# Four coupled edits to a fused two-layer kernel: segment 0's attention by halves of its queries, two of its row tiles normed midway, memory sums by 32-column products, narrower masked k, and a new order

## The chip, the cores and the metric

The kernel runs on one core of one Trainium2 chip. The metric is the device time in microseconds; lower is better. Three runs of the kernel before gave 544.15, 544.17 and 544.77 us, so the median is 544.17 us. One more execution was profiled.

Names used below: PE is the tensor engine (PEld its weight loads), DVE the vector engine, ACT the scalar engine, POOL the GpSimd engine, SP the sync engine, which issues most DMAs. `us` is a microsecond.

## The reference, cut to what matters

Two layers of the same kind are run over 2048 rows of 512. Each is an attention with a compressive memory, and a gated feed-forward.

```python
def _A_ref(x, wq, wk, wv, wo, beta):          # H = 32 heads of 16, N = 4 segments of L = 512
    ...
    for s in range(N):
        logits = einsum('bhqd,bhkd->bhqk', qs, ks) * scale + mask      # causal inside the segment
        a_dot = einsum('bhqk,bhkd->bhqd', softmax(logits), vs)
        pq = phi(qs)                                                   # t + 1 for t > 0, else exp(t)
        a_mem = einsum('bhld,bhde->bhle', pq, M) / (einsum('bhld,bhd->bhl', pq, z)[..., None] + 1e-06)
        outs.append(g * a_mem + (1.0 - g) * a_dot)
        pk = phi(ks)
        M = M + einsum('bhld,bhle->bhde', pk, vs)
        z = z + einsum('bhld->bhd', pk)
    ...
    return o @ wo
def _B_ref(x, w_gate, w_up, w_down):
    return _gelu(x @ w_gate) * (x @ w_up) @ w_down
x = x + _A_ref(_layernorm(x), ...)
x = x + _B_ref(_layernorm(x), ...)
x = x + _A_ref(_layernorm(x), ...)
x = x + _B_ref(_layernorm(x), ...)
```

M is a 16 by 16 matrix for each head, so it is used block by block along a diagonal.

## The kernel before

**Steps.** `k` counts eight steps: k = 0 to 3 are the segments of the first layer, 4 to 7 those of the second. Step k has an `Att(k)` and an `Ffn(k)`. Segment k + 4 needs the feed-forward of step k, and memory goes from one segment to the next, so attention of later segments runs beside the feed-forward of earlier ones. All weights and x stay in SBUF.

**Attention.** Rows are normed (`Norm`): statistics of each of four row tiles (`st6`, `mv`), one scale for all four on POOL (`rs`), the normed tile `xn`, and its transpose into `xnT`, either by PE (`turn_item`, tiles in `BY_PE`) or by a DMA transpose on SP's queue. Projections give q, k (`kf`) and v, v with a column for the softmax's denominator (`vaug`). The 32 heads are four blocks `b` of eight; a block's heads of even and odd number (`par`) are told apart by masked copies of k, `kx` (`masked_copies`, L417 on DVE or POOL). Scores are taken in nine rounds for each block (`round_of`, `FULL`, `PAIRED`), 36 for each step, by row tiles of PE (L938). One exponential on ACT (L1398, 128x1024) serves two rounds' half; POOL masks the diagonal. A `flush_item` sums probabilities times v by column tiles of PE (L954) for one block and one parity. Behind it DVE turns the result (`byq`, L971), takes the reciprocal (`r`), scales (`ab`, L979), turns it back (`aT`, L986) and, from the second segment on, adds the part from memory (`amT`). When the four blocks are there, 16 products with `wo` are added to x (L1027), and the rows are normed again for the feed-forward (`xnTf`).

**Memory.** phi(k) is made on ACT, POOL and DVE (`e`, L745) and turned by DMA (`phik`). `upd_item` sums phi(k) times v: 16 products of 128 rows by 128 columns, of which only the blocks on the diagonal are used. DVE then multiplies by a mask `bd` into `mblk` and keeps the running sum in `macc`. The next segment takes `den` (`zcols`, 16 products 8 wide) and `num` (`mblk`, 16 products 128 wide) from it, scales (`am`, L820) and turns by DMA (`amT`).

**Feed-forward.** 14 tiles of `wg` (gate), gelu on ACT, 14 of `wu` (up), times gelu on DVE (L1092), and 14 products for each of four row tiles with `wd` (down), added to x. `gel_sb` also serves as `vaug` of step 0, and `wd_sb` holds q, k and masked k of step 0 until `w_down` is loaded over them; so the first gate tiles wait for step 0's memory sum, and seven loads of `wd` wait for step 0's scores.

**Order.** Every engine runs a fixed list of instructions. `order` writes it when the program is built: it keeps a clock for each engine, picks PE's next piece of work among the items that it believes ready by their due times, and posts the work that follows to DVE, ACT, POOL and SP. `POLICY` holds the weights of these choices. Where it finds nothing for PE it puts in a product of the constant tile `warm` (L476 or L471 with `warm`), and `FILL` such narrow products (L584) go ahead of each transpose by PE. Nothing of this is decided on the chip: there the engines only wait for each other's semaphores.

**Tiling modes of PE.** A product may use the whole array (128\*128), four column tiles (128\*32, four instructions side by side) or four row tiles (32\*128). `product` cuts a dense product into four column tiles when a flush stands near.

Of the kernel before, what the change touches and what calls it, by code (L numbers as in the profile page):

```python
# [12 lines left out]
ALU = mybir.AluOpType  # L13
# [18 lines left out]
VALUES = TPS * VW + 16  # L32
SCALE = DH ** -0.5
# [11 lines left out]
PAIRED = [(ki, P * ki, C, C * ki) for ki in range(TPS)]  # L45


def round_of(t):

    b, i = divmod(t, ROUNDS)  # L50
    if i == SHARED:
        return b, (0, 1), PAIRED, None
    par = int(i > SHARED)
    return b, (par,), FULL[i - par * (SHARED + 1)], DIAG[i - par * (SHARED + 1)]


BY_PE = {("xnTf", 0), ("xnTf", 1), ("xnTf", NK - 1)}
BANKS = 8
# [3 lines left out]
URGENT, SOON, NORMAL = -4.0, -1.5, 0.0  # L62
XN_BUFS = 4
BUFS = 6
FILL = 2
# [4 lines left out]
    flush_wait=31.348, piece_slack=5.108, kb_slack=25.115, mem_slack=-15.103, margin=2.314, qk_due=0.572,  # L70
    e_q=-1.218, e_k=1.714, exp_slack=-25.107, e_slack=9.023, phi_slack=17.383, gelu_slack=6.274,
    act_evict=8.464, first_evict=0.965, gate_step=0.061, up_due=-0.553, up_step=0.062, down_due=2.078,
    down_step=0.526, upd_due=0.786, kb_act=6.552, vz_slack=-10.454, x_dve=-0.565, v0_due=-1.4, x1_at=-45.234,
    x2_at=18.289, x3_at=24.819, x3_load=-3.83, direct=4, gelu_tiles=4, look=1.769, lag=0.5, wv_at=8.591,
    xn_pool=7.037, kb_pool=5.303, cut_pool=1.107, at_pool=10.661, pe_turns=2, gate_due=0.765, shun=0.534,
    col_gap=3.33, hold=8, early=4.123, starve=0.308, near=-1.576, cap=4, soon=9.685, columns=0)
# [15 lines left out]
class Engine:  # L92
# [24 lines left out]
    def serve(self, now):  # L117
# [9 lines left out]
        job = min((j for j in jobs if j[0] + self.LATENCY <= start + 0.03), key=lambda j: j[0] + j[1] + (  # L127
# [123 lines left out]
class Item:  # L251


    def __init__(self, due, ready, ops, done, kind, ps, after="start"):
        self.after = after
        self.due = due if callable(due) else lambda: due
        self.ready, self.ops, self.done, self.kind, self.ps = ready, ops, done, kind, ps
        self.posted = 0.0
# [27 lines left out]
def order(pol, nc, cst, seg, wrk, psp, A_x, A_wq, A_wk, A_wv, A_wo, A_beta, B_x, B_w_gate, B_w_up, B_w_down, out):  # L286
# [88 lines left out]

    tmp_e2 = cst.tile([P, H], F32, name="tmp_e2")
    cden = cst.tile([P, H], BF16, name="cden")
    macc = cst.tile([P, 4, P], F32, name="macc")
# [32 lines left out]
    def masked_copies(ready, slack, kx, kf, told):  # L411
# [4 lines left out]
        def vector(which, eng):  # L416
            return lambda: eng.tensor_scalar(out=kx[:, :, C * which:C * which + P], in0=kf, scalar1=masks[:, which:which + 1],  # L417
                                             scalar2=None, op0=ALU.mult)
# [6 lines left out]
        ck.dve.post(ready, slack, (Port(0.35), vector(0, nc.vector), None),  # L425
                    (Port(0.35), vector(1, nc.vector), told), taken=taken)
        ck.pool.post(ready, slack + pol.kb_pool, (Port(1.57, True), vector(0, nc.gpsimd), None),
# [50 lines left out]
    def soon(name, n=KT, part=1.0):  # L478

        t = ck.pe - 0.1 - ck.back  # L480
# [20 lines left out]
    class Norm:  # L501
        def __init__(self, key, tt0, tag, slack, free):
            self.key, self.tt0, self.tag, self.slack, self.free = key, tt0, tag, slack, free
            self.mv, self.n, self.left = None, 0, TPS
# [3 lines left out]

        def stats(self, j, ready):
            def emit():  # L510
                if self.mv is None:
                    self.mv = self.small("mv", 2)
# [3 lines left out]
            def told(t):  # L516
                self.n += 1
                if self.n == TPS:
                    self.scales(t)

            ck.dve.post(ready, self.slack, (0.66, emit, None),
                        (0.17, lambda: nc.vector.bn_aggr(out=self.mv[:, j, :], in_=self.st6[:]), told))  # L522

        def scales(self, ready):
            def first():
                self.ve = wrk.tile([P, TPS, 1], F32, tag="lnve", name="ve")
                nc.gpsimd.tensor_scalar(out=self.ve[:], in0=self.mv[:, :, 1:2], scalar1=EPS_LN, scalar2=None,
                                        op0=ALU.add)

            def second():  # L530
                self.rs = self.small("rs", 1)
                nc.gpsimd.tensor_tensor(out=self.rs[:], in0=self.ve[:], in1=mhalf[:], op=ALU.pow)  # L532

            ck.pool.post(ready, URGENT, (0.25, first, None),
                         (1.05, second, lambda t: ck.when(self.free, lambda: self.start(max(t, ck.pe)))))

        def start(self, ready):
            self.xnT = seg.tile([P, KT, L], BF16, tag=self.tag, bufs=1, name="xnT")
            for j in range(TPS):
                xn_slots.take(lambda n, j=j: bufs.take(lambda i: self.row(j, n, i, max(ready, ck.pe))))  # L540

        def normed(self, j, i, eng=nc.vector):
            xn = buffer(i, "xn")
            eng.tensor_scalar(out=xn[:], in0=x_sb[:, self.tt0 + j, :], scalar1=self.mv[:, j, 0:1],  # L544
# [3 lines left out]
        def row(self, j, n, i, ready):  # L548
# [13 lines left out]
            def told(t):  # L562
                if self.by_pe():
                    items.append(self.turn_item(j, xn, t, landed))
                else:
                    turn_later(t, self.slack, lambda: self.xnT[:, :, j * P:(j + 1) * P], lambda: xn()[:], landed,
                           pol.margin)

            on_dve_or_pool(ready, self.slack, pol.xn_pool if self.key[0] == "xnTa" else None, Port(0.405),
# [5 lines left out]
        def turn_item(self, j, xn, t, landed):  # L575
# [4 lines left out]
            def turned():  # L580
# [8 lines left out]
                        lambda: evict(ps, lambda: self.xnT[:, :, j * P:(j + 1) * P], turned, landed, URGENT),  # L589
# [937 lines left out]
```

## Time and profile before

| what | us |
|---|---|
| median of three runs | 544.17 |
| span of the profiled execution | 542.6 |
| PE busy | 527.1 |
| DVE busy | 443.1 |
| ACT busy | 434.4 |
| POOL busy | 305.9 |

How to read the rows that follow: a timeline row is start, duration, engine, line, operation, out<-in with rows\*columns of PE's tile and the moving operand's shape, and the count of merged instructions; in brackets stands idle time before it and what ended it. A group row has the count, then total busy us and mean ns of one, then the idle time before. A row of the view by stretch has the stretch, its length, and for each engine busy us and (x) instructions. The profiled execution's span leaves out what lies around the program's instructions, which the timed runs hold.

### The profile page before, as it was taken

To read this page: it belongs to the slowest core of one execution; us is meant where nothing else is said; L and a number is where in the kernel's file an instruction comes from. 1 tells how busy PE (TensorE), PEld (TensorE's weight loads), DVE (VectorE), ACT (ScalarE), POOL (GpSimd) and SP (SyncE) were. 2 spreads that over 40 slices of the span, in tenths; PEclk is the share of its full clock that TensorE was granted. 3 is DMA by queue.
4 is the path that set the end of the run, shared out by engine and by line. 5 is a ranking of instruction groups with operands and counts; after the bars stand their busy time and mean duration, and the time that the engine had idled before them with its cause. 6 is when DMAs were issued, how large, how long until landed. Compare 5 with 4: busy or idle time off the path is not lost.

```text
span 542.6 us, 21272 instructions
## 1 busy us (share of the span) xinstructions
PE 527.1 (97%) x9271; PEld 274.9 (51%) x9332; DVE 443.1 (82%) x816; ACT 434.4 (80%) x540; POOL 305.9 (56%) x359
## 2 busy tenths in 40 slices
PE   8999989999999999999999999999999999999997
PEld 4454455454545444544544555545465456555444
DVE  7898999799988999879987998889586797786342
ACT  6999989988998989989799798996879977930320
POOL 4897786369846788349993468716753265300000
PEclk9999999999999999999999999999999999999999
DMA  8306510610331123310312250211420105100001
GB/s 268 98 13 192 117 23 17 171 35 20 51 50 24 24 40 61 41 38 9 41 32 50 33 71 4 40 33 23 79 52 3 22 13 89 24 3 25 16 0 40
DMA packets 64784, 26.94 MB, mean 50 GB/s; under 512 B 49074, under 2 KB 64690, under 8 KB 64690
## 3 DMA queue, kind: packets, MB, share of 16 engines
q1 hardware_dynamic: 64400, 25.31, 22.7%
q8 instruction: 73, 1.20, 0.9%
q10 hardware_dynamic: 290, 0.26, 0.2%
q14 instruction: 21, 0.17, 0.1%
HBM read 9.70 MB, written 2.10 MB: 22 GB/s over the span
## 4 chain that ended last, share of the span: by engine, by line
PE 83%; DVE 12%; issue 2%; DMA 2%; ACT 0%; POOL 0%; SPq 0%; DVEq 0%; ACTq 0%
PE ps L476 44%; PE ps L471 25%; PE ps L938 7%; PE ps L954 6%; DVE st L514 2%; DVE x_sb L1027 1%; DVE xn L544 1%; DVE byq L971 1%; DMA phik<-e 1%; DVE phiq L745 1%; DVE mv L522 1%; DMA x_sb<-in_A_x_dram 0%; DMA amT<-am 0%; DVE e L745 0%; ACT pt L1398 0%
## 5 line engine op out<-in xcount | busy, mean ns | idle before, releaser
L1398 ACT ACTIVATE pt<-ps 128x1024 bf16<-128x1024 f32 x288 | 279.1, 1026 | 44.3 <-PE ps L938 40.3
L1345 POOL TENSOR_SCALAR_AFFINE_SELECT pt<-pt 128x256 bf16<-128x256 bf16 (+1 forms) x192 | 108.6, 579 | 117.1 <-ACT pt L1398 110.4
L1092 DVE TENSOR_TENSOR gel_sb<-gel_sb,ps 128x512 bf16<-128x512 bf16 x112 | 75.2, 681 | 34.0 <-PE ps L476 25.0
L476 PE MATMUL ps<-xnT,wu_sb 128*128 128x512 bf16 x287 | 66.8, 379 | 1.4 <-issue 1.1
L476 PE MATMUL ps<-xnT,wg_sb 128*128 128x512 bf16 x261 | 62.6, 379 | 1.3 <-issue 0.5
L764 POOL TENSOR_SCALAR e<-e 128x512 bf16<-128x512 bf16 x37 | 57.6, 1557 | 1.6 <-ACT e L741 0.6
L971 DVE STREAM_TRANSPOSE byq<-ps 128x512 f32<-128x512 f32 x64 | 45.0, 706 | 16.3 <-PE ps L954 15.6
L476 PE MATMUL ps<-wd_sb,gel_sb 128*128 128x512 bf16 (+1 forms) x293 | 56.8, 340 | 1.3 <-issue 1.0
L1027 DVE TENSOR_TENSOR x_sb<-x_sb,ps 128x512 bf16<-128x512 bf16 (+1 forms) x68 | 42.8, 640 | 16.5 <-PE ps L476 14.8
L1350 POOL TENSOR_SCALAR_AFFINE_SELECT pt<-pt 64x1024 bf16<-64x1024 bf16 x40 | 47.7, 1194 | 15.1 <-ACT pt L1398 13.8
L471 PE MATMUL ps<-wd_sb,gel_sb 128*32 128x512 bf16 (+1 forms) x792 | 47.1, 378 | 0.6 <-issue 0.6
L476 PEld LDWEIGHTS <-wu_sb 128*128 128x128 bf16 x301 | 28.3, 98 | 33.8 <-issue 0.7
L471 PE MATMUL ps<-xnT,wg_sb 128*32 128x512 bf16 x700 | 42.4, 380 | 0.1
L514 DVE BATCH_NORM_STATS2 st<-x_sb 128x6 f32<-128x512 bf16 x60 | 40.4, 673 | 0.1
L476 PEld LDWEIGHTS <-wg_sb 128*128 128x128 bf16 x273 | 25.3, 98 | 29.1 <-DVE byq L971 0.6
L476 PEld LDWEIGHTS <-gel_sb 128*128 128x128 bf16 x306 | 28.3, 98 | 22.6 <-issue 1.1
L954 PE MATMUL ps<-pt,vaug 128*32 128x256 bf16 (+2 forms) x1344 | 34.8, 238 | 0.3 <-POOL pt L1345 0.3
L471 PE MATMUL ps<-xnT,wu_sb 128*32 128x512 bf16 x588 | 34.1, 379 | 0.0
L417 POOL TENSOR_SCALAR kx<-kf,masks 128x512 bf16<-128x512 bf16 x20 | 33.0, 1649 | 1.2
L1151 ACT ACTIVATE gel_sb<-gel_sb 128x2048 bf16<-128x2048 bf16 (+1 forms) x21 | 33.2, 1643 | 0.0
L954 PEld LDWEIGHTS <-vaug 128*32 128x32 bf16 x1344 | 27.9, 97 | 10.5 <-issue 2.3
L544 DVE TENSOR_SCALAR xn<-x_sb,mv,rs 128x512 bf16<-128x512 bf16 x58 | 31.4, 592 | 2.2 <-POOL rs L532 1.9
(149 smaller groups left out, 877.0 us busy)
## 6 DMA issues: line engine op xcount, KB each, us to landing
vz<-vaug SPq DMA_DIRECT2D x14, 136.0 KB, 2.7
wg_sb<-in_B_w_gate_dram SPq DMA_DIRECT2D x8, 224.0 KB, 4.0
wu_sb<-in_B_w_up_dram SPq DMA_DIRECT2D x8, 224.0 KB, 5.0
wd_sb<-in_B_w_down_dram SPq DMA_DIRECT2D x7, 256.0 KB, 4.7
x_sb<-in_A_x_dram SPq DMA_DIRECT2D x3, 512.0 KB, 6.6
out_dram<-x_sb SPq DMA_DIRECT2D x12, 128.0 KB, 1.9
xnT<-xn SPq DMA_TRANSPOSE x40, 2.5
wk_sb<-in_A_wk_dram SPq DMA_DIRECT2D x2, 256.0 KB, 5.1
```

The source lines that it names most:

```text
L471: nc.tensor.matmul(out[r], lhsT=lhsT[:, r], rhs=rhs, start=start, stop=stop, tile_position=(0, 32 * c))
L476: nc.tensor.matmul(out, lhsT=lhsT, rhs=rhs, start=start, stop=stop)
L514: nc.vector.bn_stats(out=self.st6[:, 0, :], in_=x_sb[:, self.tt0 + j, :])
L764: lambda eng: eng.tensor_scalar(out=e[0][:], in0=e[0][:], scalar1=1.0, scalar2=None, op0=ALU.min), summed)
L938: nc.tensor.matmul(ps_all[:, bank, o + c0:o + c0 + n], lhsT=lhsT, rhs=self.q[rows, b, q0:q0 + n], start=True, stop=True, tile_position=(32 ...
L954: nc.tensor.matmul(ps()[32 * j:32 * j + 32, q0:q0 + n], lhsT=va[:, ki * VW + g:ki * VW + g + 32], rhs=pt_all[:, places[i], j, c0:c0 + n], ...
L971: nc.vector.transpose(out=self.byq[:, par, :, :].rearrange("p a c -> p (a c)"), in_=ps()[:])
L1027: ck.dve.post(ck.made(), slack, (0.15 + 0.00104 * (c1 - c0), lambda: nc.vector.tensor_tensor(out=xt, in0=xt, in1=ps()[:, 0:c1 - c0], op=AL ...
L1092: ck.dve.post(ck.made(), NORMAL, (0.683, lambda: nc.vector.tensor_tensor(out=g, in0=g, in1=ps()[:], op=ALU.mult), lambda t: (ps.read(t), e ...
L1345: nc.gpsimd.affine_select(out=view, in_=view, pattern=[[0, 4], [0, n], [1, C]], compare_op=ALU.is_ge, fill=0.0, base=C, channel_multiplier=-1)
L1350: nc.gpsimd.affine_select(out=view, in_=view, pattern=[[0, 4 * TPS], [1, C]], compare_op=ALU.is_ge, fill=0.0, base=0, channel_multiplier=-1)
L1398: nc.scalar.activation(out=pt_all[:, s0:s0 + 2, 2 * p:2 * p + 2, :].rearrange("p r h c -> p h r c"), in_=ps_all[:, pair[0]:pair[1] + 1, :] ...
```

## The change

1. **Segment 0's attention by halves of its queries** (`HALVED`, `table`). Block 0 is done as before. For blocks 1 to 3 the rounds are laid out anew: first the rounds whose queries are in the first 256 rows (`early`), then those of the second 256 (`late`), in the order of blocks 1, 2, 3 and 3, 1, 2; rounds of the pair of parities are shared between blocks. A flush now covers both parities of one block and one half, and its steps on DVE behind the whole turn are half as wide. `wo` of row tiles 0 and 1 needs the first halves alone (`aTh`).
2. **Two of its four tiles normed midway** (`QUICK`, `told`, `scales`). For the feed-forward of step 0, tiles 0 and 1 get their scale, `xn` and transposes as soon as the two are there, tiles 2 and 3 later. Tile 2 takes its mean from an accumulated row sum of the addition to x, and its variance from a square on ACT (`added`).
3. **Memory sums by 32-column products** (`upd_item`). For each of the 16 pairs of row tile and block, four products with 32 columns of phi(k) and 32 columns of v, side by side in the column tiles. `macc` shrinks to 32 columns a block; `spread` makes `mblk` out of it. In the first segment `macc` is now copied ahead of `mblk`, where `mblk` came straight from PSUM.
4. **Narrower masked k** (`masked_copies`). The first masked copy on DVE and POOL is 64 columns a tile, not 128; the other 64 were written over by the second.
5. **New order.** All values of `POLICY` are new (among them `margin`, which adds to the expected landing of a DMA transpose: 2.314 before, 0.058 now), `FILL` is 0, a priority `CHAIN` stands ahead of all others for step 0's last flush and the norms behind it, and gate tiles that do not share memory with step 0's v may be taken before its memory sum.

```diff
-PAIRED = [(ki, P * ki, C, C * ki) for ki in range(TPS)]
...
-def round_of(t):
...
-    b, i = divmod(t, ROUNDS)
...
+HALVED = (0,)
+BOTH = (0, 1)
+EARLY = [(1, 192, 64, 0), (0, 64, 192, 64)]
+LATE = [([(3, 448, 64, 0), (2, 320, 192, 64)], 2), ([(0, 256, 256, 0)], 0), ([(1, 256, 256, 0)], 0)]
...
+    def early(b):
+        return [([(b, (par,), *piece) for piece in EARLY], 2) for par in range(2)]
+
+    def late(b):
+        return [([(b, (par,), *piece) for piece in pieces], n) for pieces, n in LATE for par in range(2)]
+
+    for b in range(1 if halved else KT):
+        got, parts = whole_block(b)
+        at = add(got)
+        units.append((b, None, [((par,), [at[i] for i in range(i0, i1)]) for par, i0, i1 in parts]))
+    if halved:
+        a1, s12, a2 = add(early(1)), add([(shared((1, 0), (1, 1), (2, 0), (2, 1)), None)]), add(early(2))
+        a3, s3 = add(early(3)), add([(shared(*((3, ki) for ki in range(TPS))), None)])
+        units += [(1, 0, [(BOTH, [*a1, *s12])]), (2, 0, [(BOTH, [*a2, *s12])]), (3, 0, [(BOTH, [*a3, *s3])])]
+        units.append((3, 1, [(BOTH, [*s3, *add(late(3))])]))
+        l1 = add(late(1))
+        s12 = add([(shared((1, 2), (1, 3), (2, 2), (2, 3)), None)])
+        units += [(1, 1, [(BOTH, [*l1, *s12])]), (2, 1, [(BOTH, [*s12, *add(late(2))])])]
...
+QUICK = {("xnTf", k): (2,) for k in HALVED}
...
 XN_BUFS = 4
 BUFS = 6
...
-    flush_wait=31.348, piece_slack=5.108, kb_slack=25.115, mem_slack=-15.103, margin=2.314, qk_due=0.572,
...
+    flush_wait=3.781, piece_slack=153.679, kb_slack=116.912, mem_slack=-48.48, margin=0.058, qk_due=1.192,
...
-    macc = cst.tile([P, 4, P], F32, name="macc")
+    macc = cst.tile([P, 4, 32], F32, name="macc")
...
-            return lambda: eng.tensor_scalar(out=kx[:, :, C * which:C * which + P], in0=kf, scalar1=masks[:, which:which + 1],
-                                             scalar2=None, op0=ALU.mult)
+            n = P if which else C
+            return lambda: eng.tensor_scalar(out=kx[:, :, C * which:C * which + n], in0=kf[:, :, 0:n],
+                                             scalar1=masks[:, which:which + 1], scalar2=None, op0=ALU.mult)
...
+        def told(self, j):
+            def fn(t):
+                self.n += 1
+                if self.quick:
+                    self.pairs[j // 2] += 1
+                    if self.pairs[j // 2] == 2:
+                        self.scales(t, j // 2 * 2, 2)
+                elif self.n == TPS:
+                    self.scales(t, 0, TPS)
...
+            def add():
+                self.moments()
+                made.append(wrk.tile([P, 1], F32, tag="rowsum", bufs=4, name="rowsum"))
+                nc.vector.scalar_tensor_tensor(out=xt, in0=ps()[:], scalar=1.0, in1=xt, op0=ALU.mult, op1=ALU.add,
+                                               accum_out=made[0][:])
+
+            def mean():
+                nc.vector.tensor_tensor(out=self.mv[:, j, 0:2], in0=made[0][:].to_broadcast([P, 2]), in1=means[:], op=ALU.mult)
+
+            def square():
+                nc.scalar.activation(out=junk[:], in_=xt, func=ACT.Square, scale=float(D) ** -0.5, bias=self.mv[:, j, 0:1],
+                                     accum_out=self.mv[:, j, 2:3])
+
+            ck.dve.post(ck.made(), slack, (0.76, add, ps.read), (0.15, mean, lambda t: ck.act.post(
+                t, slack, (0.95, square, self.told(j)), table="exp")))
...
-            def m(c):
-                j, b = divmod(c, 4)
-                product(blocks()[:, b, :], self.phik[:, j, b * P:(b + 1) * P],
-                        by_head(self.vaug)[:, j, 4 * b:4 * b + 4, :, 0:DH], c == 0, c == n_mm - 1)
+            def m(j, b):
+                ck.tiling("columns")
+                for c in range(4):
+                    nc.tensor.matmul(pairs()[32 * c:32 * c + 32, b, :], lhsT=self.phik[:, j, b * P + 32 * c:b * P + 32 * c + 32],
+                                     rhs=by_head(self.vaug)[:, j, 4 * b + c, :, 0:DH], start=(j == b == 0),
+                                     stop=(j == TPS - 1 and b == 3), tile_position=(0, 32 * c))
...
+                def spread():
+                    nc.vector.tensor_tensor(out=made[0][:].rearrange("p b (c d) -> p b c d", d=32),
+                                            in0=macc[:].unsqueeze(2).to_broadcast([P, 4, 4, 32]),
+                                            in1=bd[:].rearrange("p (c d) -> p c d", d=32).unsqueeze(1).to_broadcast([P, 4, 4, 32]),
+                                            op=ALU.mult)
...
-                    steps = [(0.154, lambda: nc.vector.tensor_copy(out=zacc[:], in_=self.zk[:]), kept),
-                             (0.683, gated(blocks), None),
-                             (Port(0.2), z, told),
-                             (0.683, lambda: nc.vector.tensor_copy(out=macc[:], in_=blocks()), psm.read)]
+                    first = [(0.283, lambda: nc.vector.tensor_copy(out=macc[:], in_=pairs()), psm.read),
+                             (0.154, lambda: nc.vector.tensor_copy(out=zacc[:], in_=self.zk[:]), kept)]
...
+                ck.dve.chain(ck.made(), pol.mem_slack, *first, (Port(0.69), spread, None), (Port(0.2), z, told))
...
+            u, b, h, n, pars, used = flush
...
+            c0, c1 = (0, L) if h is None else (half * h, half * h + half)
+            na = (c1 - c0) // 32
+            work = []
+            for par in pars:
+                for t in used:
+                    for b2, par2, ki, q0, nq, o in TABLES[k][0][t][0]:
+                        if b2 == b and par in par2 and c0 <= q0 < c1:
+                            work.append((par, t, vz if len(par2) > 1 else self.vaug, ki, q0 - c0 + (par * half if h is not None else 0),
+                                         nq, o))
+            work.sort(key=lambda w: (w[0], w[3] if h is not None else w[2] is vz))
...
-                    nc.vector.transpose(out=self.byq[:, par, :, :].rearrange("p a c -> p (a c)"), in_=ps()[:])
+                    nc.vector.transpose(out=(self.byq[:, pars[0], :, :].rearrange("p a c -> p (a c)") if h is None else
+                                             self.byq[:].rearrange("p u a c -> p (u a c)")[:, 0:2 * na * 32]), in_=ps()[:])
...
-                    nc.vector.transpose(out=self.aT[:, b, :], in_=self.ab[b][:].rearrange("p a c -> p (a c)"))
+                    nc.vector.transpose(out=self.aT[:, b, c0:c1], in_=made[0][:, 0:na, :].rearrange("p a c -> p (a c)"))
...
-                return Item(k + 0.61 + 0.001 * j, lambda: soon(("aT", k)),
-                            dense(ps, pairs), done, kind="wo", ps=ps, after=("aT", k, 3))
+                return Item(k + 0.61 + 0.001 * j, lambda: soon(("aTh", k, j // 2), eager=k in HALVED),
+                            dense(ps, pairs), done, kind="wo", ps=ps, after=("aTh", k, j // 2, 3))
...
-                            lambda: ck.has(("xnTf", k)) and (("down", k - 1) if k else ("upd", 0)) in ev,
+                return Item(lambda: -0.8 if phase[0] == k else k + pol.gate_due + pol.gate_step * place(ft),
+                            lambda: ck.has(("xnTf", k)) and (k == 0 and ft >= HELD or (("down", k - 1) if k else ("upd", 0)) in ev),
```

One line of `POLICY` stands for all of them.

More of the change, by code (lines that the diff above doesn't have):

```diff
@@ L528, in first @@
                                         op0=ALU.add)
             def second():
[L531 to L539, printed above, removed]
+                if self.rs is None:
+                    self.rs = self.small("rs", 1)
@@ L1447, in order @@
                 got = [it for it in items if it.after in ev and it.ready() and (
-                    it.kind != "flush" or not streams or tight() or it.posted < late or ck.mode == "columns")]
+                    it.kind != "flush" or it.chain or not streams or tight() or it.posted < late or ck.mode == "columns")]
                 if got:
```

251 lines of the change are left out of this document (150 added, 101 removed).

## The prediction

> **What bounds the kernel now.** I read the page first: shares of the engines, the granted clock, the chain that ended last.
>
> ```profile
> span 542.6 us, 21272 instructions
> ...
> PE 527.1 (97%) x9271; PEld 274.9 (51%) x9332; DVE 443.1 (82%) x816; ACT 434.4 (80%) x540; POOL 305.9 (56%) x359
> ...
> PEclk9999999999999999999999999999999999999999
> ...
> PE 83%; DVE 12%; issue 2%; DMA 2%; ACT 0%; POOL 0%; SPq 0%; DVEq 0%; ACTq 0%
> ```
>
> TensorE is busy 97% of the span at the full granted clock, and 83% of the chain is PE. So the time is PE's instruction stream, plus the places where that stream waits. The second view, busy time by stretch, says where those are (columns: the stretch, then PE, PEld, DVE, ACT, POOL busy, the clock, DMA).
>
> ```profile
> 60.00:80.00 20.00, 17.89 (x426) 10.61 (x426) 19.49 (x41) 17.40 (x23) 15.63 (x18) 1.00 0.23 36
> ...
> 100.00:120.00 20.00, 19.48 (x408) 10.48 (x405) 19.23 (x36) 17.30 (x23) 9.85 (x13) 1.00 0.42 108
> 120.00:140.00 20.00, 18.35 (x365) 9.75 (x361) 19.53 (x39) 17.20 (x23) 17.40 (x20) 1.00 0.07 16
> ...
> 160.00:380.00 220.00, 216.83 (x4183) 110.96 (x4207) 192.39 (x343) 195.97 (x239) 140.77 (x160) 1.00 0.21 35
> ...
> 539.00:542.60 3.60, 0.46 (x5) 0.17 (x2) 0.42 (x1) 0.00 (x0) 0.00 (x0) 0.99 0.13 36
> ```
>
> From 160 to 380 us PE idles 3.17 of 220 us, 0.29 per 20, which is the ground level. It idles 2.11 us in 60 to 80, 0.52 in 100 to 120 and 1.65 in 120 to 140, and there DVE is nearly full. Only there can a better order win anything. The third view, PE's timeline, shows the first of these places.
>
> ```profile
> 70.74 0.28 PE L476 MATMUL ps<-gel_sb,phik 128*128 128x128 bf16 x2
> 71.38 0.60 PE L476 MATMUL ps<-gel_sb,phik 128*128 128x128 bf16 x7 [0.35 <-DMA phik<-e]
> ...
> 73.82 0.20 PE L938 MATMUL ps<-q,kf 16*128 16x64 bf16 x2
> 74.39 0.40 PE L938 MATMUL ps<-q,kf 16*128 16x64 bf16 x10 [0.37 <-ACT pt L1398]
> 74.72 0.51 PE L476 MATMUL ps<-warm 128*128 128x128 bf16 x6
> 75.16 0.52 PE L954 MATMUL ps<-pt,vaug 128*32 128x256 bf16 x16
> 76.00 0.30 PE L954 MATMUL ps<-pt,vaug 128*32 128x64 bf16 x8 [0.33 <-POOL pt L1345]
> ...
> 76.50 0.20 PE L938 MATMUL ps<-q,kf 16*128 16x64 bf16 x3
> 77.16 0.27 PE L938 MATMUL ps<-q,kf 16*128 16x64 bf16 x5 [0.45 <-DVE macc L893]
> ...
> 77.71 0.21 PE L584 MATMUL ps<-warm 128*128 128x32 bf16 x2
> 77.76 0.38 PE L586 MATMUL ps<-ident,xn 128*128 128x128 bf16 x4
> ```
>
> Segment 0's attention is done, its feed-forward needs the normed rows, and PE is filled with products of `warm`. Read from start to start (a record's own length hides part of a wait), the four breaks are worth about 0.5 to 0.6 us each; with the smaller ones the stretch loses 3.3 us. The stretch from 100 to 160, read the same way, loses 3.0. Sum 6.3 us, beside 29 whole-width `warm` products (0.22 us of wait for each; 0.17 in the first place alone).
>
> **The change, part by part.** PE's price list comes from four places of its timeline.
>
> ```profile
> 230.70 1.67 PE L476 MATMUL ps<-xnT,wu_sb 128*128 128x512 bf16 x7 [0.16 <-issue]
> 232.31 0.40 PE L938 MATMUL ps<-q,kx 32*128 32x256 bf16 x12
> 232.64 2.12 PE L476 MATMUL ps<-xnT,wu_sb 128*128 128x512 bf16 x9
> ...
> 288.41 0.69 PE L471 MATMUL ps<-zcols,phiq 128*32 128x8 bf16 x64
> 288.93 1.27 PE L471 MATMUL ps<-xnT,wu_sb 128*32 128x512 bf16 x20
> ...
> 395.11 1.19 PE L471 MATMUL ps<-vaug,phik 128*32 128x128 bf16 x64
> 396.07 0.65 PE L471 MATMUL ps<-wd_sb,gel_sb 128*32 128x512 bf16 x7
> ```
>
> *Memory sums.* Now 16 products, 128 wide, take 396.07 - 395.11 = 0.96 us. After it is 64 products of 32 columns of phi(k) with 32 columns of v, four at a time. The nearest row is `zcols`: 64 such products, 8 wide, in 0.52 us. So 0.5 each, and six sums save 6 x 0.46 = 2.8 us. Ends: 0.24 (the time of now by the columns, 128 to 32) and 0.96 (nothing saved): 4.3 to 0.
>
> [...]
>
> *Mode switches.* Every change between whole, column and row tiles costs time. 230.70 to 232.31 is seven products of 0.216 and 0.10; 232.31 to 232.64 is 0.22 of scores and 0.11. The changed kernel's instructions stand in 322 runs of one mode against 304: 18 x 0.11 = 2.0 us more (fewer dense products are cut into columns, since flushes stand differently).
>
> *Fills.* 31 `warm` products become 25, and the 24 narrow ones ahead of the transposes (`FILL`) go. 74.72 to 75.16 is six of them and a switch: 0.055 each; 77.71 to 77.76 is two narrow ones: 0.03 each. 6 x 0.055 + 24 x 0.03 = 1.0 us less.
>
> PE without waits: -2.8 + 2.0 - 1.0 = **-1.8 us**. The other columns streamed are the same in number.
>
> *Halved attention of segment 0.* Six units of half the queries take the place of three whole ones: as many turns of a whole bank, three more reciprocals, scales and turns back of half the size. This adds some 1.3 us to DVE beside PE's projections and is free there; without that cover it costs what it is. On the path is only the last unit.
>
> ```profile
> 62.59 0.70 DVE L971 STREAM_TRANSPOSE byq<-ps 128x512 f32<-128x512 f32 x1
> 63.32 0.35 DVE L975 RECIPROCAL r<-byq 128x32 f32<-128x32 f32 x1
> 63.71 0.69 DVE L979 TENSOR_TENSOR ab<-byq,r 128x512 bf16<-128x512 f32 x1
> 64.43 0.71 DVE L986 STREAM_TRANSPOSE aT<-ab 128x512 bf16<-128x512 bf16 x1
> ...
> L1199 ACT ACTIVATE pt<-x_sb,shift 128x512 bf16<-128x512 bf16 x1 | 0.7, 721 | 0.0
> ...
> L417 POOL TENSOR_SCALAR kx<-kf,masks 128x512 bf16<-128x512 bf16 x20 | 33.0, 1649 | 1.2
> ```
>
> That is 2.55 us now, and about 1.9 with the last three steps halved. In the changed order eight `wo` products stand before the last flush, and 2.2 us of other PE work between it and the other eight. So `wo` stops waiting. Tiles 0 and 1 are normed while PE still projects segment 3; only tile 3's statistics stay on DVE at the end, and tile 2's variance moves to ACT (0.72 by the row of the same operation at the start; at worst one exponential of 1.03 ahead of it). From the last `wo` to the first `wg` product there are 5.7 us of work in the changed order, against 7.3 now, 1.3 of it fills. I take 0.4 us of remaining wait (0 to 1.5). Of the 3.3 us lost there, 2.9 go.
>
> *Where the stall goes.* The 25 fills of the new order all stand in one place: behind the last `wd` product of the first feed-forward, ahead of segment 4's v products (the next layer), which are drawn forward into a hole. These v products wait for `xnT` of segment 4. In DVE's new order 13 instructions stand between the turn of segment 1's last flush but one and the first `xn` of it: the last add to x, its two of statistics, two of phi, the memory sum's four, a whole turn, reciprocal, scale, turn back. DVE does one in 0.53 us in the 100 to 120 stretch (19.23 / 36). With `xn`, and 0.3 left of the turn when the last `wd` product ends, that is 14 x 0.53 + 0.3 = 7.7 us; then one transpose by DMA, whose landing is on the page:
>
> ```profile
> xnT<-xn SPq DMA_TRANSPOSE x40, 2.5
> ...
> phik<-e SPq DMA_TRANSPOSE x24, 3.4
> ...
> wd_sb<-in_B_w_down_dram SPq DMA_DIRECT2D x7, 256.0 KB, 4.7
> ...
> L971 DVE STREAM_TRANSPOSE byq<-ps 128x512 f32<-128x512 f32 x64 | 45.0, 706 | 16.3 <-PE ps L954 15.6
> ...
> L745 DVE SCALAR_TENSOR_TENSOR phiq<-q,e 128x512 bf16<-128x512 bf16 x24 | 19.2, 807 | 0.4 <-POOL e L764 0.4
> ...
> L878 DVE TENSOR_TENSOR mblk<-macc,bd 128x512 bf16<-128x512 f32 x4 | 3.9, 970 | 0.0
> ```
>
> 7.7 + 2.5 = 10.2, plus 0.6 for the memory sum's own wait for `phik`, against 5.8 us of PE work in that place: 5.0 us of wait. Behind the v products stand a flush, segment 1's `wo` and segment 4's q and k, so all wait together. Ends: 0.17 us for each fill gives 4.2; if all the steps took as long as the three large kinds above (0.83 on average), 11.9 + 3.1 - 5.8 = 9.2. I stay near the lower end, since statistics, sums and reciprocals are short. The 3.0 us lost there before are part of this.
>
> *Small new waits.* The order keeps less room before DMA landings: segment 2's first gate product stands 13.2 us of PE work after its last `wo`, now 15.9. The last four loads of `wd` stand on SP's queue behind two transposes of `amT`, and the products that read them follow 8 to 10 us of PE work after those that the transposes wait for; such a load takes 4.7 us to land, after some 4 us of scaling and issuing. The first memory block has one more copy ahead of it on DVE. I take 0.8 us for these (0 to 3).
>
> *Free:* the masked k copies, 256 wide for 512 in the first half. POOL's 1.65 us (row above) becomes about 0.9; POOL is busy 56%, and only scores that stand later read them. A copy that were waited for would gain 0.7.
>
> Sum: -1.8 + (0.4 + 5.0 + 0.8) - 6.3 = **-1.9 us** on the profiled execution. Its span is 542.6; the runs' median of 544.17 has 1.6 us around it, and the tail behind the last product (the 3.6 us of the last stretch) is untouched. Forecast 544.2 - 1.9 = **542.3 us**.
>
> **The rivals.**
> - *The waits shrink more* (540.5): 4.2 us in the new hole, none elsewhere but 0.2: -1.8 + 4.4 - 6.3 = -3.7. For it: 160 to 380 shows how well a fixed order can run. Against: DVE is full there.
> - *What the order gains is given back* (544.6): 1.5 us of wait left at segment 0 and 2 us of small ones: -1.8 + 1.5 + 5.0 + 2.0 - 6.3 = +0.4. For it: DVE is not relieved, and gates still need all four tiles normed.
> - *The new hole grows* (546.7): DVE's chain before segment 4's `xn` at 0.77 us a step. The wait is then 0.3 + 10.8 + 3.1 - 5.8 = 8.4 us, `wd` comes 1 us late: -1.8 + 8.4 + 0.4 + 1.8 - 6.3 = +2.5. It decides from 8 us in that one place. For it: 0.81 and 0.97 in the rows above.
> [...]
>
> **How the numbers follow.** Forecast 0.40, more gain 0.25, given back 0.18, hole grows 0.15, narrow products 0.02. What a measurement can tell from no change is about 0.2%, 1.1 us: faster is below 543.1, slower above 545.3. Faster takes nearly all of the first (0.38), the second, and 0.03 of the third: 0.66. Slower takes 0.11 of the fourth, the fifth, and 0.02 of the third: 0.15. Same is the rest, 0.19. The range, 539.0 to 545.8, leaves out the far end of the gain and of the growing hole.
>
> **What would show it.** Right: a column-tiled memory sum in 0.5 us; 322 runs of one mode with 0.11 between; PE's idle time in 60 to 80 near the ground level; one hole of 4 to 6 us between 115 and 130 with DVE full. Wrong: narrow sums at 1 us; waits at the first `wg` or `wd` products; idle time over 0.5 us per 20 after 160.

## The result, and the profile after

The changed kernel takes 565.15 us (median of four runs, 564.73 to 566.54), the kernel before 544.16 us in the same session. The ratio is 1.0386, 95% interval 1.0374 to 1.0399: slower by 21 us, where 1.9 us less had been forecast. The profiled execution took 564.73 us, its span is 563.0. Its page, in the order of the lines shown of before (span, busy time, clock, engines of the chain):

```profile
span 563.0 us, 21401 instructions
...
PE 528.5 (94%) x9330; PEld 271.3 (48%) x9401; DVE 442.8 (79%) x834; ACT 432.4 (77%) x528; POOL 299.7 (53%) x353
...
PEclk9999999997899999999999999999999999999999
...
PE 65%; POOL 10%; DVE 9%; issue 7%; ACT 6%; DMA 2%; SPq 0%; POOLq 0%; ACTq 0%; DVEq 0%
```

PE's busy time grew by 1.4 us only, its idle time from 15.5 (542.6 - 527.1) to 34.5 us (563.0 - 528.5). PE's share of the chain fell from 83% to 65%, and POOL, which had none, now has 10%. The clock's row has a 7 and an 8, where before it was full to the end. The stretches of the prediction, and three around the dip of the clock (same columns: length, PE, PEld, DVE, ACT, POOL, clock, DMA):

```profile
60.00:80.00 20.00, 18.59 (x272) 9.21 (x275) 16.85 (x37) 17.27 (x25) 11.77 (x13) 1.00 0.17 38
...
100.00:120.00 20.00, 18.61 (x345) 9.11 (x348) 15.38 (x31) 16.40 (x20) 12.56 (x16) 1.00 0.43 100
120.00:140.00 20.00, 14.75 (x395) 8.77 (x393) 18.15 (x33) 14.90 (x17) 15.31 (x18) 0.84 0.23 35
...
160.00:380.00 220.00, 211.48 (x4093) 107.31 (x4120) 187.40 (x339) 192.13 (x227) 139.00 (x155) 1.00 0.21 37
...
126.60:130.00 3.40, 1.39 (x36) 0.64 (x28) 2.84 (x6) 2.93 (x4) 3.24 (x4) 1.00 0.61 43
130.00:133.40 3.40, 3.24 (x141) 2.40 (x141) 2.31 (x5) 1.94 (x2) 2.31 (x3) 0.51 0.02 5
133.40:136.80 3.40, 1.97 (x50) 1.27 (x47) 3.37 (x6) 3.24 (x4) 1.84 (x3) 0.99 0.38 82
136.80:143.60 6.80, 4.84 (x78) 2.58 (x82) 4.04 (x7) 4.96 (x7) 4.61 (x7) 0.51 0.50 61
```

Two things are new. From 160 to 380 us, where PE idled 0.29 us per 20, it now idles 8.52 of 220, 0.77 per 20: the loss is spread over the kernel. And in 120 to 140 PE idles 5.25 us, and between 130 and 144 us PE runs at half clock for 10.2 us in all. What PE waits for stands in the view of waits (engine, line, releaser, us, times, longest):

```profile
PEld L1061 <- issue: 19.6, 37, 2.0
...
PE ps L1061 <- POOL pt L1481: 8.0, 8, 1.8
...
PE ps L961 <- DMA phik<-e: 2.0, 1, 2.0
```

L1061 is the flush, L1481 POOL's mask of a round that both parities share; two of them, one for each half of the partitions, cover a round. L961 is the memory sum. (The line of PEld is idle time of the weight loads for which the profile shows no releaser; nothing below rests on it.) Before, one flush (there L954) waited for POOL, and this is the only such line:

```profile
PE ps L954 <- POOL pt L1345: 0.3, 1, 0.3
```

Read from start to start against the prediction's price list (a matmul's own length hides part of a wait), nine flushes wait 10.3 us for that mask. All waits of PE, with what the half clock adds, are as follows (from some 9,300 starts each, so the last digit is rough; for the 3.5 of before in 60 to 80 the prediction had 3.3):

| stretch, us | before | after |
|---|---|---|
| 0 to 20 | 3.3 | 3.5 |
| 20 to 60 | 0.7 | 2.6 |
| 60 to 80 | 3.5 | 2.0 |
| 80 to 100 | 0.1 | 1.5 |
| 100 to 160 | 3.0 | 12.3 |
| 160 to 380 | 0.4 | 8.2 |
| behind 380 | 1.0 | 4.6 |
| sum | 12.2 | 34.6 |

The 22 us more are the loss. Without waits the list of products costs 2.0 us less than before, by the same prices. The masks are the largest part of the loss, but not all of it: of the 8.2 us in 160 to 380 some 2.7 are waits for the mask. Among the others there a score product stands 0.77 us for DVE (at 237.75 us), and two products in the middle of their runs stand 0.80 us each with no releaser that the profile shows (273.79 and 344.85). One of the nine flushes, first on PE's timeline, then POOL's, then ACT's:

```profile
445.65 1.67 PE L527 MATMUL ps<-xnT,wu_sb 128*128 128x512 bf16 x7
447.26 0.40 PE L1032 MATMUL ps<-q,kx 32*128 32x64 bf16 x12
447.59 0.63 PE L1061 MATMUL ps<-pt,vaug 128*32 128x256 bf16 x24
449.51 0.30 PE L1061 MATMUL ps<-pt,vz 128*32 128x64 bf16 x16 [1.30 <-POOL pt L1481]
449.63 1.92 PE L522 MATMUL ps<-xnT,wu_sb 128*32 128x512 bf16 x32
```
```profile
447.11 2.35 POOL L1481 TENSOR_SCALAR_AFFINE_SELECT pt<-pt 64x1024 bf16<-64x1024 bf16 x2 [9.87 <-ACT pt L1527]
```
```profile
445.05 1.94 ACT L1527 ACTIVATE pt<-ps 128x1024 bf16<-128x1024 f32 x2
```

The exponentials of the shared round end at 446.99 us, POOL masks from 447.11 to 449.46, and PE has been at the flush since 447.59. Its first 24 products run; the 16 that read the shared round stand until 449.51, and dense products of the kind that ran ahead of the flush stand behind them.

### The profile page after: what moved, and what is told of

Read it like the earlier page. It is cut to its first block, busy times and chain, and to the rows that moved or that the text cites. A ratio compares the mean times of both kernels' runs of the same rounds, so it can differ in the third digit from the quotient of the medians.

```text
span 563.0 us, 21401 instructions
## 1 busy us (share of the span) xinstructions
PE 528.5 (94%) x9330; PEld 271.3 (48%) x9401; DVE 442.8 (79%) x834; ACT 432.4 (77%) x528; POOL 299.7 (53%) x353
## 4 chain that ended last, share of the span: by engine, by line
PE 65%; POOL 10%; DVE 9%; issue 7%; ACT 6%; DMA 2%; SPq 0%; POOLq 0%; ACTq 0%; DVEq 0%
PE ps L527 34%; PE ps L522 19%; PE ps L1032 6%; PE ps L1061 5%; ACT pt L1527 4%; POOL pt L1481 3%; POOL pt L1476 2%; POOL kx L468 2%; DVE st L588 2%; DVE x_sb L1152 1%; POOL xn L638 1%; DVE byq L1080 1%; DMA phik<-e 1%; DMA wd_sb<-in_B_w_down_dram 1%; POOL rs L625 1%
## 5 line engine op out<-in xcount | busy, mean ns | idle before, releaser
L1476 POOL TENSOR_SCALAR_AFFINE_SELECT pt<-pt 128x256 bf16<-128x256 bf16 (+1 forms) x186 | 109.9, 604 | 130.9 <-ACT pt L1527 126.2
L1223 DVE TENSOR_TENSOR gel_sb<-gel_sb,ps 128x512 bf16<-128x512 bf16 x112 | 73.8, 681 | 42.0 <-PE ps L527 24.0
L527 PE MATMUL ps<-xnT,wg_sb 128*128 128x512 bf16 x269 | 63.9, 379 | 1.7 <-issue 1.4
L859 POOL TENSOR_SCALAR e<-e 128x512 bf16<-128x512 bf16 x38 | 59.8, 1578 | 8.1 <-ACT e L836 7.0
L527 PE MATMUL ps<-wd_sb,gel_sb 128*128 128x512 bf16 (+1 forms) x297 | 59.1, 345 | 2.7 <-issue 1.6
L1080 DVE STREAM_TRANSPOSE byq<-ps 128x512 f32<-128x512 f32 x64 | 45.2, 708 | 17.0 <-PE ps L1061 15.5
L1481 POOL TENSOR_SCALAR_AFFINE_SELECT pt<-pt 64x1024 bf16<-64x1024 bf16 x34 | 41.2, 1212 | 22.9 <-ACT pt L1527 21.8
L522 PE MATMUL ps<-wd_sb,gel_sb 128*32 128x512 bf16 (+1 forms) x772 | 45.4, 371 | 0.8 <-issue 0.8
L522 PE MATMUL ps<-xnT,wg_sb 128*32 128x512 bf16 x660 | 40.4, 380 | 0.3 <-DMA xnT<-xn 0.3
L468 POOL TENSOR_SCALAR kx<-kf,masks 128x256 bf16<-128x256 bf16 (+1 forms) x28 | 36.2, 1301 | 0.0
L1061 PE MATMUL ps<-pt,vaug 128*32 128x256 bf16 (+2 forms) x1344 | 35.9, 242 | 0.0
L1061 PEld LDWEIGHTS <-vaug 128*32 128x32 bf16 x1344 | 28.2, 98 | 14.0 <-issue 6.9
L1032 PE MATMUL ps<-q,kx 32*128 32x64 bf16 (+2 forms) x1120 | 31.4, 219 | 2.8 <-issue 1.1
```

The lines of the kernel that those rows point to most:

```text
L522: nc.tensor.matmul(out[r], lhsT=lhsT[:, r], rhs=rhs, start=start, stop=stop, tile_position=(0, 32 * c))
L527: nc.tensor.matmul(out, lhsT=lhsT, rhs=rhs, start=start, stop=stop)
L859: lambda eng: eng.tensor_scalar(out=e[0][:], in0=e[0][:], scalar1=1.0, scalar2=None, op0=ALU.min), summed)
L1032: nc.tensor.matmul(ps_all[:, bank, o + c0:o + c0 + n], lhsT=lhsT, rhs=self.q[rows, b, q0:q0 + n], start=True, stop=True, tile_position=(32 ...
L1061: nc.tensor.matmul(ps()[32 * j:32 * j + 32, q0:q0 + nq], lhsT=va[:, ki * VW + g:ki * VW + g + 32], rhs=pt_all[:, places[t], j, o:o + nq], ...
L1080: nc.vector.transpose(out=(self.byq[:, pars[0], :, :].rearrange("p a c -> p (a c)") if h is None else self.byq[:].rearrange("p u a c -> p ...
```

## The experiments

**The numbers of POLICY, or the structure.** The first run puts the old numbers under the new structure, the second the new numbers under the old structure.

```diff
 # old_weights: the changed kernel
-FILL = 0
+FILL = 2
...
-    flush_wait=3.781, piece_slack=153.679, kb_slack=116.912, mem_slack=-48.48, margin=0.058, qk_due=1.192,
+    flush_wait=31.348, piece_slack=5.108, kb_slack=25.115, mem_slack=-15.103, margin=2.314, qk_due=0.572,
...
 # new_weights: the kernel before, with the same lines the other way round
```

> The changed kernel with the numbers of POLICY and FILL of before: the halves, the narrow sums and the narrow copies stay, the order comes from the old numbers. By the instructions, PE without waits stands at 525.9 us, as before (523.9 in the changed kernel). Theory (the new numbers let the order open products before their inputs are there, and the waits come from that): the 22 us of new wait go, 541 to 547 us, and vz products that wait over 0.3 us for POOL's mask of 64x1024 become one or none instead of nine. Rival (the edits of the structure cost it, halves above all): 558 us or more, with the hole behind the first feed-forward still there.

> The kernel before with the numbers of POLICY and FILL of after: no halves, no narrow sums, wide copies. By the instructions, PE without waits stands at 527.4 us, 1.6 over before. Theory (the new numbers): PE waits again, 20 to 40 us of it in all, 555 to 575 us, with vz products behind POOL's mask among the waits. Rival (the structure): 544 to 549 us.

Measured: 551.43 us with the old numbers (ratio to before 1.0139, 1.0124 to 1.0155) and 569.68 us for the old structure with the new ones (1.0474, 1.0454 to 1.0494). Both lie on the theory's side, the first 4 us above its range. The first run's view of waits has no flush behind POOL any more; in that of the second run, POOL's mask (there L1350) stands high among what PE waits for:

```profile
PE ps L954 <- POOL pt L1350: 11.4, 11, 1.5
```

So the new numbers cost the old structure 25.5 us, and account for 14 of the new structure's 21. The old ones, which were in use with another list of items, do not serve the new structure well either: PE still waits 19.6 us in all.

**The waits taken away with the order held.** The order is written when the program is built, from prices that stand in the code. So an operation can be made shorter without moving any other, if its price is left.

```diff
 # short_mask
-        view = pt_all[C * h:C * h + C, slot, :, :].rearrange("p u (t c) -> p (u t) c", c=C)
+        view = pt_all[C * h:C * h + C, slot, 0:1, 0:C]
-        nc.gpsimd.affine_select(out=view, in_=view, pattern=[[0, 4 * TPS], [1, C]], compare_op=ALU.is_ge,
+        nc.gpsimd.affine_select(out=view, in_=view, pattern=[[0, 1], [1, C]], compare_op=ALU.is_ge,
 # wide_fill
-                product(ps()[:, 0:P], warm[:], wide[:, 0, :])
+                product(ps()[:, 0:L], warm[:], wide[:, 0:4, :])
 # short_wide: both
```

The short mask covers 64 of the 1024 columns and leaves the other 960 unmasked, so these two kernels tell of time alone.

> The changed kernel in exactly its own order, but POOL's two masks of a shared round cover 64 of the 1024 columns each; the rest stays unmasked. Theory (nine flushes wait for the second of these masks, 10.3 us in sum): each mask is some 0.8 us shorter, so nearly all nine waits end; 552 to 557 us. Rival (the exponential, or the eviction, is as late as the mask, or the time is lost in the structure): 562 us or more, the vz products waiting for ACT instead.

> The changed kernel in its own order, but each of the 25 fills streams 512 columns instead of 128, 0.216 us for 0.055: 4.0 us more PE work, put where PE mostly waits. Theory (the clock granted 0.5 for 10.2 us between 130 and 144 us is an answer to PE standing idle there): the clock stays nearer to 1.0, and up to 5.1 us come back; 560 to 564 us. Rival (the clock falls whatever PE does there, or the waits alone set the time): the half clock stays, 564 to 568 us.

> The changed kernel in its own order, with both the short masks of POOL (64 of the 1024 columns of each shared round masked, the rest not) and the fills 512 columns wide. Theory (the waits for the masks and the half clock are two losses that add, and the short masks alone gained only 5.1 us because the clock was at half for longer, mean 0.981 for 0.991): the clock stays at 1.0 but for a few us, and the time is 551 to 556 us. Rival (waits that only hide one another): 557.5 to 561 us.

Measured: 560.06, 563.18 and 554.31 us. The short mask takes 294 ns for 1212 (the group of the changed kernel, then that of this run):

```profile
L1481 POOL TENSOR_SCALAR_AFFINE_SELECT pt<-pt 64x1024 bf16<-64x1024 bf16 x34 | 41.2, 1212 | 22.9 <-ACT pt L1527 21.8
...
L1481 POOL TENSOR_SCALAR_AFFINE_SELECT pt<-pt 64x64 bf16<-64x64 bf16 x34 | 10.0, 294 | 15.0 <-ACT pt L1527 13.9
```

No flush waits for it any more, but the time fell by 5.1 us, not by 8 to 13: between theory and rival. The view by stretch of that run has the rest:

```profile
126.60:130.00 3.40, 2.55 (x92) 1.47 (x84) 3.37 (x8) 3.17 (x5) 3.24 (x4) 1.00 0.59 42
130.00:133.40 3.40, 2.28 (x112) 1.90 (x116) 1.81 (x5) 1.73 (x3) 3.23 (x6) 0.59 0.03 6
133.40:136.80 3.40, 2.98 (x66) 1.78 (x58) 3.23 (x6) 3.18 (x4) 1.75 (x5) 0.50 0.38 82
136.80:143.60 6.80, 4.88 (x78) 2.60 (x83) 2.63 (x8) 6.48 (x9) 3.99 (x6) 0.50 0.30 61
```

The half clock now lasts without a break from 130.6 to 147.7 us, and there is another such stretch of 3.4 us from 86.2: 20.5 us in all for 10.2 before, which costs an estimated 5 us, half of the 10.3 more and about what is missing (at half clock products of 512 columns start 0.43 us apart, at the full clock 0.22: the changed kernel from 141.29 and from 145.70 us). With the wide fills the clock stays full in the same order, although PE has 4.0 us more work: the same stretches of that run read

```profile
126.60:130.00 3.40, 1.83 (x36) 0.67 (x28) 2.75 (x5) 2.83 (x4) 3.23 (x5) 1.00 0.67 43
130.00:133.40 3.40, 3.26 (x143) 2.09 (x144) 2.54 (x6) 2.27 (x3) 2.50 (x4) 1.00 0.09 23
```

and PE's waits in 100 to 160 fall from 12.3 to 6.6 us. At a full clock the masks are worth 563.18 - 554.31 = 8.9 us, near the 10.3 that PE waited. Together the two take 10.8 of the 21 us. This is the theory's reading; the rival (waits that hide one another) would have left 557.5 or more.

**Which number lets the flush stand too early.** A flush may be taken when each of its masks has a due time `m[0]` with `m[0] + 0.1 + ck.back <= ck.pe`, where `ck.pe` is PE's clock in `order`; `ck.back` is `lag` at the first try, 0.5 before and -83.634 in the change. A mask gets its due time when POOL's clock takes it up, so with -83.634 any mask that has one will do. The readiness of other items (`has`, `soon`) is tested with `ck.back` too, so `lag` opens more than flushes early. What is then added to `ck.pe` is the product's cost, but no wait.

```diff
 # lag_back
-    ... look=115.38, lag=-83.634, wv_at=-106.305, ...
+    ... look=115.38, lag=0.5, wv_at=-106.305, ...
 # lag_margin also
-    ... mem_slack=-48.48, margin=0.058, qk_due=1.192, ...
+    ... mem_slack=-48.48, margin=2.314, qk_due=1.192, ...
```

> The changed kernel with one number put back: lag is 0.5 again, not -83.634. So an item is opened only 0.5 us after all that it reads is due, not as soon as the job that makes it has a due time. By the instructions, PE without waits stands at 525.1 us, 1.3 over the changed kernel. Theory (lag is what lets the flushes open ahead of their masks): the nine waits of vz products for POOL's mask (10.3 us) go but for one or two, the 2 us hole behind the first feed-forward too; 547 to 556 us. Rival (another number does it, or the waits move to the next input): 558 to 567 us.

> As the last, and margin, the room that the planner adds to a transpose by DMA, 2.314 again and not 0.058. PE without waits stands at 524.5 us. Theory (both numbers take away room that the chip needs): no memory sum waits over 0.5 us for the landing of phik, 1 to 4 us under the run with lag alone. Rival (margin carries nothing, since the one wait for phik cost 2.1 us and its clock): within 1 us of it.

Measured: 554.59 and 549.61 us. With `lag` alone no flush waits for the mask of L1481, as the theory had it, and 10.6 us are gone; PE idles 0.47 us in 160 to 380. But one memory sum now waits 1.9 us for its transposed phi(k), 3.4 us at half clock behind it:

```profile
79.04 0.56 PE L961 MATMUL ps<-gel_sb,phik 128*32 128x32 bf16 x52 [1.89 <-DMA phik<-e]
```

With `margin` back too, no sum waits for phik, and 5.0 us more are gone, above the expected 1 to 4. The wait of 1.9 us and the half clock behind it (an estimated 1.7 us, half of the 3.4) make 3.6 of them; as the whole order is written anew, the rest has no single cause here. That `lag` opens flushes ahead of their masks is shown by the code, by the run with `lag` alone and by the masks' runs together; the 10.6 us are of everything that `lag` opens early, since nearly all waits in 160 to 380 go with it, not those for masks alone.

**The parts of the structure.** First the narrow sums alone, on the kernel before, in the order that its planner then writes; then the same with the old prices, which leave the order of before untouched; then the narrow copies too.

```diff
 # sums_only: upd_item and macc as in the changed kernel
 # held_sums: sixteen items at the old price, each four products; macc 32 columns wide, spread by bd as in the change
...
-                product(blocks()[:, b, :], self.phik[:, j, b * P:(b + 1) * P],
-                        by_head(self.vaug)[:, j, 4 * b:4 * b + 4, :, 0:DH], c == 0, c == n_mm - 1)
+                for i in range(4):
+                    nc.tensor.matmul(blocks()[32 * i:32 * i + 32, b, :], lhsT=self.phik[:, j, b * P + 32 * i:b * P + 32 * i + 32],
+                                     rhs=by_head(self.vaug)[:, j, 4 * b + i, :, 0:DH], start=(c == 0),
+                                     stop=(c == n_mm - 1), tile_position=(0, 32 * i))
...
 # held_sums_kx: also the narrow masked_copies, at the old price
```

> The kernel before with the narrow memory sums and their narrower macc alone; its own numbers, its own halves (none), wide copies. The order moves by itself where a sum is shorter: 312 runs of one mode for 304, 52 fills of 128 columns for 31, PE without waits at 524.8 us for 525.8. Theory (the narrow sums are a gain of 2.8 us at PE, but any order that was not fitted anew leaves some holes): 541 to 547 us. Rival (the narrow sums cost on the chip, so that the structure loses too): 548 us or more.

> The kernel before in exactly its own order (its own numbers, and the old prices for the planner), with the six memory sums as 64 products of 32 columns and the narrower macc. By the instructions, PE without waits is 2.4 us less: six sums by 0.46, less six switches more, since three sums that were whole-width products now stand between whole-width products as column tiles. Theory (the sums are the gain that was forecast, and the loss of the changed kernel, and of the narrow sums alone with an order of its own, is in the order): 541.3 to 543.0 us. Rival (the narrow sums gain nothing on the chip, or what they gain is lost in the next wait): 543.7 us or more.

> As the last, and the masked copies of k in the first half 256 wide, again in the order of before and at the old prices for the planner. PE's instructions are those of the last. Theory (the narrow copies lie beside other work): within 0.5 us of the last. Rival (scores wait for copies on POOL): up to 2 us under it.

Measured: 551.31 us for the sums in an order of their own, 541.64 us in the held order (ratio 0.9952, 0.9939 to 0.9964), 542.2 us with the narrow copies (0.9961, 0.9947 to 0.9974). The same narrow sums go with 2.6 us less or 7.0 us more, by the order that they stand in (that of the first run has 52 fills for 31 and 312 runs of one mode for 304); the first run fell on its rival's side, whose reason (the sums cost on the chip) the second refutes. One sum in the held order, start to start 0.49 us:

```profile
393.86 0.66 PE L867 MATMUL ps<-vaug,phik 128*32 128x32 bf16 x64
394.35 1.92 PE L471 MATMUL ps<-wd_sb,gel_sb 128*32 128x512 bf16 x32
```

The narrow copies gain nothing: with them the time is 0.6 us longer, just outside the 0.5 that had been expected, and the two intervals overlap. `held_sums` is the fastest version here, ahead of both kernels.

**New numbers with room in them.** With `lag` 0.5 and `margin` 2.314 held, the other numbers were chosen anew, once for the whole new structure and once, with numbers of their own, for the kernel before with the narrow sums and the narrow copies. So the second leaves out the halves, and with them the norms midway, `CHAIN` and the gate tiles ahead of the memory sum; it keeps `FILL` 2.

```diff
 # refit: the changed kernel
-    flush_wait=3.781, piece_slack=153.679, ... margin=0.058, ... lag=-83.634, ...
+    flush_wait=-17.456, piece_slack=62.236, ... margin=2.314, ... lag=0.5, ...
 # refit_whole: the kernel before, with narrow sums and copies as in the changed kernel
-    flush_wait=31.348, piece_slack=5.108, ... margin=2.314, ... lag=0.5, ...
+    flush_wait=-3.972, piece_slack=0.844, ... margin=2.314, ... lag=0.5, ...
```

> The changed kernel's structure (halves, narrow sums, narrow copies, no narrow fills) with another set of numbers, for which lag is 0.5 and margin 2.314 as before and the others were chosen anew. By the instructions, PE without waits stands at 522.3 us, in 303 runs of one mode, with 46 fills. Theory (the structure is sound and the loss was the room that lag and margin took away): no vz product waits over 1 us for POOL's mask, waits in sum 12 to 20 us for 34.6, 539 to 547 us. Rival (the halves or the narrow copies cost of themselves): 550 us or more.

> As the last without the halves: segment 0's attention by whole tiles as before, and the narrow fills kept; numbers chosen for it in the same way, lag 0.5 and margin 2.314. PE without waits stands at 521.4 us, in 298 runs. Theory (the halves are worth what they take from the stall ahead of segment 0's feed-forward, about 2 us): the stretch 60 to 80 waits 3 to 4 us here and 1 to 2 in the run with halves, and the times lie within 3 us of each other, this one the longer. Rival (the halves cost): this one is over 2 us shorter than the run with halves.

Measured: 544.04 us (ratio 1.0003, 0.9991 to 1.0016) and 543.69 us (0.9993, 0.9985 to 1.0002), PE's waits 16.3 and 16.0 us; the first one's profile is of its longest run, 546.12 us. So the structure, in an order whose numbers were chosen for it, loses nothing. But no gain of the halves is seen either: in 60 to 80 us the run with halves waits 4.7 us (3.4 us of the stretch are at half clock), the other 3.5, where 1 to 2 and 3 to 4 were expected. The end at 80 us flatters the run without halves: there the first gate product comes at 81.97 us, and PE idles 0.68 us more from 80 to 82, while with halves it comes at 76.06 us and PE idles no more. As each of the two has an order of its own, and they differ in more than the halves, what the halves are worth by themselves stays open.

## Why the prediction was wrong, step by step

- *PE without waits, -1.8 us.* Right: -2.0 by the same prices. The sum of 64 narrow products takes 0.49 us in the held order and 0.52 in the changed kernel (83.74 to 84.26 us), against 0.5. The chance of 0.02 for narrow products, the fifth of the cases, stands on a price that each of the 64 would pay by itself; no run shows such a price: 0.49 and 0.52 us for 64 are some 8 ns each, as in the `zcols` row of before (0.52 us for 64). The 322 runs of one mode were counted right.
- *Segment 0's chain, 0.4 us left of 3.3.* Right for the chain, on PE's timeline:

```profile
71.77 0.51 PE L680 MATMUL ps<-ident,xn 128*128 128x128 bf16 x6
72.11 1.03 PE L527 MATMUL ps<-wv_sb,xnT 128*128 128x512 bf16 x3
72.98 2.32 PE L527 MATMUL ps<-xnT,wg_sb 128*128 128x512 bf16 x10
```

  Neither the transposes nor the first `wg` products wait. The 2.0 us of that stretch are mainly two flushes, one behind an exponential (0.8), one behind a mask (0.6); and 1.5 us came up in 80 to 100.
- *The new hole, 5.0 us (4.2 to 9.2).* The place was right, the size wrong. It stands behind the first feed-forward, among the fills and ahead of segment 4's v products, at 127 to 144 us. It came to 12.3 us with the rest of 100 to 160: a memory sum that waits 2.1 us for phik, where 0.6 had been added, a flush that waits 2.0 us for its mask, and the half clock. The step knew DVE's chain alone, and took the clock for given: it had been 1.0 throughout before.
- *Small new waits, 0.8 us (0 to 3).* This is the step that failed most. Behind the first 20 us and outside the two places of the earlier steps the waits grew by 14.7 us: 1.9 in 20 to 60, 1.4 in 80 to 100, 7.8 in 160 to 380 and 3.6 behind. The prediction's own sign of being wrong, over 0.5 us of idle time per 20 after 160, came with 0.77. The step looked for less room ahead of DMA landings and for one copy on DVE; of that one wait came, 1.0 us of a `wd` product for its load, at 112 us, in the stretch of the new hole. It never measured, flush by flush, how much PE work stands between the scores of a shared round and the flush that reads it, against the way by ACT and POOL (two exponentials and two masks, 4.3 us in the rows above). The order has 64 flushes to ask this of, and `lag` at -83.634 stood in the new numbers. The flushes are not the whole of the 14.7 us: in 160 to 380 only some 2.7 us are theirs. The rest there are waits of other products, some with no releaser in the profile; with `lag` back nearly all of them are gone.
- *Free: the narrow copies of masked k.* Right: in the held order they gain nothing (0.6 us longer).
- *The rivals.* None had more than 2 us of waits outside the two places. "The new hole grows" (546.7) named the point from which that place decides, 8 us, and the place passed it; but it would have cost 2.5 us, an eighth of the loss.

The loss put together, with the numbers put back one after the other: 10.6 us go with `lag` and 5.0 more with `margin`. The other 5.4 go when the remaining numbers are chosen anew (544.04); no run says which of these it is. The half clock lies inside these and has no separate sum.

## What to carry to other kernels

Where the order is fixed when the program is built, every product is to be checked against the way of its latest input, engine by engine and not only for transfers: the engine that was off the critical path is the one to ask. A part of a change is priced by itself if its prices for the planner are left as they were, so that nothing else moves: 2.6 us of gain came out of what had been 7.0 us of loss in this way. And a number that lets a planner start work before its inputs are due removes the wait from the plan alone, not from the chip.

## What the runs showed of the hardware

In a stretch where PE was busy for 1.39 of 3.4 us, the clock fell to half for the next 3.4 us, and after 1.97 of 3.4 us for the next 6.8 (rows of the changed kernel above); the prediction had no such loss in any of its cases. PE's longest single wait there was 2.1 us. Fills of 512 columns for 128 kept the clock full with 1.83 of 3.4 us busy, and saved 2.0 us in spite of 4.0 us more work, and in the changed kernel itself the clock stayed full behind a stretch with 1.79 us busy of 3.4 (27.6 to 31.0). So the busy time of such a stretch alone does not say whether the clock falls, and what does stays open. Away from the ends of a run the half clock of these traces lasted 3.4 us at a time, 6.8 or, with the short masks, 17.1 us.
